# A fused attention and feed-forward kernel: first loads and copies reordered, the last block stored in two halves, and products of the unit matrix on TensorE

## The chip, the cores and the metric

The kernel runs on one core of one Trainium2 chip. That core has five engines, each with its own instruction stream in order: TensorE (PE: products, with PEld for the loads of its stationary operand), VectorE (DVE), ScalarE (ACT), GpSimd (POOL) and SyncE (SP, which here only issues DMA transfers). The metric is device time in microseconds (us) of one execution. Three runs of the kernel before gave a median of 1426.15 us (1426.09 to 1426.85).

## The reference

Attention over 8 batches, 8 heads, 576 positions and 64 features, with a threshold on the scores, and then a two-layer feed-forward network over the 4608 rows of 512 features:

```python
scores = scale * np.matmul(q, k.transpose(0, 1, 3, 2))
thresh = np.max(scores, axis=-1, keepdims=True) - tau
scores = np.where(scores >= thresh, scores, -1000000000.0)
...
attn = attn / (np.sum(attn, axis=-1, keepdims=True) + 1e-09)
return np.matmul(attn, v).astype(np.float32)
...
h = x @ w_in
g = np.maximum(h, 0.0) + np.log1p(np.exp(-np.abs(h)))
return (g @ w_out).astype(np.float32)
```

All of it is in float32; the two weight matrices (512 x 2048 and 2048 x 512) are given in float64. On TensorE a float32 value is carried as a sum of a high and a low part, so that most products are made three times (high by high, high by low, low by high).

## The kernel before, in words

Attention goes in 32 units, one for each batch and pair of heads, and each unit in nine tiles of 128 rows (288 tiles, numbered g). For a unit the kernel loads k, q and v (`load`, `load_v`), splits k and q into parts (`split_k`, `split_q`, with the helpers `hi_of` and `lo_of`), transposes them on PE (`qkT`, L375 to L383) and copies them from PSUM: keys into `kT`, queries, scaled by `qscale`, into `qT[0]` (`queries`, L396). `qT[1]` holds the same with its two halves of 64 partitions exchanged: by two DVE copies in the first unit (L401), by two DMA transfers in all others (`swap`, L404 and L405). The last 64 rows of each head go through `qkT_rest` and `qm`.

A tile's steps are: `scores` (PE, L442), `row_max` (DVE), `exps` (ACT), `mask` (DVE: the threshold and the row's sum), `weights_T` (PE: transposes of the masked exponentials, L490 to L496), `weights_hi` (ACT) and `weights_lo` (DVE) from PSUM into SBUF, and the products with v (`values`). Tiles before `TG` = 36 transpose into banks of the pool `ps_g`, which has four; later ones into the scores' own bank. The first five units take v whole (L568), the others in parts (L574 to L576).

Beside attention, `prep` converts the weights: each of 32 pieces is loaded (L204, tile `wc_i` or `wc_o`), then ACT takes its absolute value (`first`, L212, tile `wa_i` or `wa_o`), POOL and DVE make float32 of its words, and POOL splits it. One piece is begun every second tile. From tile 41 on, the feed-forward network (`hidden`, L664 to L668; `softplus`; `project`, L732) runs between the steps of the tiles, at a quota for each, in nine chunks of 512 rows; behind the last tile only feed-forward work is left. `project_out` adds a block of 128 rows and 512 columns to its sum on DVE, and `store_out` issues its store on SP (L764).

The order is written out by hand. A string gives the steps of each tile, `PAT0` before tile 36 and `PAT` after; in it T is `weights_T`, h `weights_hi`, l `weights_lo`, R `row_max`, e `exps`, m `mask`, f a part of the feed-forward work, x the preparation of the next unit, S `scores`, v the products of `slow`, w the weights, and p a point. `defer(n, f)` holds a function back for n points. All this gives the order in which instructions are made. A planner then sets the order on each engine by priority (the earlier made, the higher) and by when it reckons each instruction to be ready, so that an instruction can be put ahead of earlier ones; `behind(i, others)` adds an edge that keeps i after the last of `others`.

Of the kernel before, what the change touches and what calls it, by code (L numbers as in the profile page):

```python
# [23 lines left out]
P = 128  # L24
# [8 lines left out]
LAG0 = 5  # L33
PAT = "ThRlefmpfxSvwp"
PAT0 = "RMTeShlfpfxvwp"
WD = 4
ST = (1, 3, 4, 4, 5, 6, 6, 8)
VO = (1, 1, 1, 0)
# [22 lines left out]
def tile_kernel(ctx: ExitStack, tc: tile.TileContext, q, k, v, tau, w_in, w_out, out):  # L61
# [29 lines left out]

    nc.scalar.preload_act_table_set("exp_and_others")

    ones = apool.tile([P, S], F32, tag="R", bufs=1, name="ones")[:, 0:P]
# [7 lines left out]
    tau_sb = cpool.tile([P, 1], F32, name="tau_sb")  # L102
    nc.sync.dma_start(tau_sb, tau.partition_broadcast(P))
    ntau = cpool.tile([P, 1], F32, name="ntau")
    nc.vector.tensor_scalar(out=ntau, in0=tau_sb, scalar1=-1.0, scalar2=None, op0=ALU.mult)
    nc.vector.tensor_tensor(out=ntau, in0=ntau, in1=tau_sb, op=ALU.min)
    qscale = cpool.tile([P, 1], F32, name="qscale")
    nc.vector.tensor_scalar(out=qscale, in0=tau_sb, scalar1=0.0, scalar2=SCALE,
                            op0=ALU.is_ge, op1=ALU.mult)

# [11 lines left out]
    nc.vector.memset(qm.bitcast(F32), 0.0)  # L122

    def hi_of(eng, out_, in_):
        if eng is nc.gpsimd:
            eng.tensor_scalar(out=out_, in0=in_, scalar1=1.0, scalar2=1.0, op0=ALU.mult, op1=ALU.mult)
        elif eng is act:
            eng.copy(out_, in_)
        else:
            eng.tensor_copy(out_, in_)  # L130

    def lo_of(eng, out_, in_, hi):
        eng.tensor_tensor(out=out_, in0=in_, in1=hi.bitcast(F32), op=ALU.subtract)  # L133

# [4 lines left out]
    now = {"p": 0, "tile": 0}  # L139
    masked = []  # L140
    scored = []

    def behind(i, others):
# [25 lines left out]
    def to_f32(src, want, name, then):  # L169
# [124 lines left out]
    for b in range(B):  # L294
        for kind in (("one", "two") if b < NSPLIT else ("all",)):
            for hp in range(NPAIR):
# [17 lines left out]
                units.append(s)  # L314

    def load(s):
        h0 = 2 * s.hp
        s.kn = apool.tile([P, 10, D], F32, tag="nat", bufs=3, name=f"kn_{s.i}")
        s.qn = apool.tile([P, 10, D], F32, tag="nat", bufs=3, name=f"qn_{s.i}")
        for t, src in ((s.kn, k), (s.qn, q)):  # L320
            load_rows(s, t, src)
            if t is s.qn and s.kind == "one":
                continue
            for j in range(2):
                nc.sync.dma_start(t[j * SR:(j + 1) * SR, NC, :], src[s.b, h0 + j, SM:S, :])

    def load_rows(s, t, src):
        nc.sync.dma_start(
            t.rearrange("p (h s) d -> p h (s d)", h=2)[:, :, 0:NC * D],
            src[s.b, 2 * s.hp:2 * s.hp + 2, 0:SM, :].rearrange("h (p c) d -> p h (c d)", c=NC),  # L330
        )

    def load_v(s):
        if s.whole:
            s.vn = apool.tile([P, 10, D], F32, tag="vt", bufs=3, name=f"vn_{s.i}")
        else:
            s.vn = apool.tile([P, 10, D], F32, tag="nat", bufs=3, name=f"vn_{s.i}")
        load_rows(s, s.vn, v)
# [12 lines left out]
    def split_q(s, j):  # L351
        t = apool.tile([P, NC + 1, 2 * D], F32R, tag="q2", bufs=1, name=f"q2_{s.i}_{j}")
        a, z = s.cols.start, s.cols.stop
        if j == 0 and s.kind != "one":
            z += 1
        qj = s.qn[:, j * (NC + 1) + a:j * (NC + 1) + z, :]
        hi_of(s.eng, t[:, a:z, 0:D], qj)
        lo_of(s.eng_lo, t[:, a:z, D:2 * D], qj, t[:, a:z, 0:D])
        s.q2.append(t)
# [10 lines left out]
    def qkT(s, j, n):  # L370
# [10 lines left out]
        for c in cols:  # L381
            src = s.k2[:, j * (NC + 1) + c, :] if n == 0 else s.q2[j][:, c, :]
            nc.tensor.transpose(pr[:, c * P:(c + 1) * P], src, identr)  # L383
        if n == 0:
            s.kT.append(apool.tile([P, S + SR], F32R, tag="kT", name=f"kT_{s.i}_{j}"))
            t = s.kT[j]
            defer(1, lambda: act.copy(t[:, SR:S], ps))
# [6 lines left out]
    def queries(s, t0, t1, ps):  # L394

        act.activation(t0, ps, AF.Copy, scale=qscale)  # L396
        if s.i:
            swap(t0, t1)
            return
        for i, o in ((slice(0, D), slice(D, P)), (slice(D, P), slice(0, D))):  # L400
            vec.tensor_scalar(out=t1[o], in0=ps[i], scalar1=qscale[i], scalar2=None, op0=ALU.mult)  # L401

# [4 lines left out]
    def qkT_rest(s, j, ps):  # L407

        act.copy(
            s.kT[j].rearrange("p (k n) -> p k n", n=SR)[:, 0:NC * 2 + 2:NC * 2 + 1, :],  # L410
            ps[:, j * SR:(j + 1) * SR].unsqueeze(1).to_broadcast([P, 2, SR]),
        )
        if j == 0 and s.kind != "one":
            for m in range(2):
                act.activation(qm[:, 0, m, m * SR:(m + 1) * SR], ps[:, P + m * SR:P + (m + 1) * SR],
                                     AF.Copy, scale=qscale)
            swap(qm[:, 0], qm[:, 1])

# [6 lines left out]
    def scores(s, t):  # L425
# [14 lines left out]
        for m, (lhs, j) in enumerate(parts):  # L440
            for hf in range(2):
                i = nc.tensor.matmul(sp[:, hf, 0:HS], lhs, s.kT[j][:, k0 + hf * HS:k0 + (hf + 1) * HS],  # L442
                                     start=(m == 0), stop=(m == len(parts) - 1))
        scored.append(i)

    def row_max(s, t):
# [6 lines left out]
    def exps(s, t):  # L453
        act.activation(e_all[:, s.half[t], :].rearrange("p (h n) -> p h n", h=2), s.sp[t][:, :, 0:HS],
                             AF.Exp, bias=s.m[t][0], scale=1.0)

    def mask(s, t):
# [12 lines left out]
    def mate(s, t):  # L470
# [4 lines left out]
        return (t + 1, False) if u % 2 == 0 else (t - 1, True)  # L475

    def weights_T(s, t):
        half = s.half[t]
# [72 lines left out]
    def slow_products():  # L551
        if not slow:
            return
        for f in slow[0][:3]:
            behind(f(), scored)
        del slow[0][:3]
# [163 lines left out]
    def project(u, qt, tb):  # L720
        o = ps_g.tile([P, 512], F32, tag="g", name=f"o_{u.n}_{qt}_{tb}")
# [5 lines left out]
        for n, (i, m) in enumerate(steps):  # L727
# [4 lines left out]
            nc.tensor.matmul(o, u.g[fc][m // 2][:, sl], wo[fc][:, m % 2, :], start=(n == 0), stop=(n == 3 * QF - 1))  # L732
            if n == 3 * QF - 1:
                defer(1, lambda: project_out(u, qt, tb, o))
            if (u.n, qt, tb) in early and n == 3 * PAIR - 1:
# [3 lines left out]

    def project_out(u, qt, tb, o):  # L740
        if qt == 0 and tb % 2 == 0:
# [3 lines left out]
        if qt == 0:  # L745
            act.copy(a, o)
        else:
            vec.tensor_tensor(out=a, in0=o, in1=a, op=ALU.add)
        if qt == NFC // QF - 1:
            defer(1, lambda: store_out(u, tb, a))  # L750

    def store_out(u, tb, a):
        t0 = u.t0 + tb * P
        c = 0
        while c < P:
# [5 lines left out]
            else:  # L761
                m = min(S - o, P - c)
                dst = out[b * S + o:b * S + o + m, :]
            nc.sync.dma_start(dst, a[c:c + m, :])  # L764
            c += m
# [187 lines left out]
    u0.eng, u0.eng_lo = eng, nc.gpsimd  # L953
    scores(*tiles[0])
    row_max(*tiles[0])
    exps(*tiles[0])
# [83 lines left out]
```

## Time and profile before

| | us |
|---|---|
| median of three runs | 1426.15 |
| the profiled execution, its own time | 1425.26 |
| its span, first to last instruction | 1423.5 |
| PE busy | 1380.4 |
| DVE busy | 987.5 |
| ACT busy | 846.7 |
| POOL busy | 586.2 |

The profile is of one execution. An engine's busy time is the union of its instructions; PE's products overlap, so that a busy PE is not a PE at its peak, and its rate is read from the distance between the starts of like products. A row of a timeline gives the start and the length in us, the engine, the line, the operation, the tiles written and read, their shapes, a count of instructions merged, and in brackets how long the engine sat idle before and what ended that. Most ACT and DVE instructions carry L156 and most POOL ones L126 or L133, the lines of helpers, and are told apart by their tiles.

### The profile page before, as it was taken

The page shows a single profiled execution, that of the slowest core. Times are in us where ns is not written, and L with a number is a line of the kernel's source. Part 1 is how long each engine was busy: PE and PEld are TensorE (multiplying, and loading weights), DVE is VectorE, ACT ScalarE, POOL GpSimd, SP SyncE. Part 2 cuts the span into 40 slices and gives each one's busy share as a digit, 9 for nine tenths or more (in the row PEclk, how much of TensorE's full clock was granted, in tenths as well). Part 3 has the DMA queues.
Part 4 walks back from the last instruction along what each step waited for, and adds up shares of the span by engine and source line. Part 5 has one row for each costly group of instructions (what it writes and reads, how often), then busy time and mean ns, then how long its engine had stood idle before and what let it go on. Part 6 is the DMA issues. An engine that isn't in the chain of part 4 may idle for free.

```text
span 1423.5 us, 23587 instructions
## 1 busy us (share of the span) xinstructions
PE 1380.4 (97%) x7860; PEld 1164.5 (82%) x7860; DVE 987.5 (69%) x2211; ACT 846.7 (59%) x1615; POOL 586.2 (41%) x619
## 2 busy tenths in 40 slices
PE   6987999999999999999999999999999999999998
PEld 5555688788888888888888888888888888788886
DVE  6988688787777777787778777877777777402111
ACT  5766767667666576667666666667666765221110
POOL 3666666543333433344334333344334431323221
PEclk9999999999999999999999999999999999999999
DMA  5766766435333534445443533453434532343421
GB/s 168 220 191 208 233 195 186 125 102 173 111 105 111 156 105 124 120 131 158 118 119 98 158 108 110 124 145 117 123 113 141 154 94 84 110 130 115 135 76 45
DMA packets 131209, 189.94 MB, mean 133 GB/s; under 512 B 35312, under 2 KB 86800, under 8 KB 131088
## 3 DMA queue, kind: packets, MB, share of 16 engines
q1 hardware_dynamic: 131088, 188.43, 45.4%
q8 instruction: 63, 1.03, 0.3%
q14 instruction: 58, 0.48, 0.1%
HBM read 140.51 MB, written 27.41 MB: 118 GB/s over the span
## 4 chain that ended last, share of the span: by engine, by line
PE 86%; DVE 4%; DMA 2%; issue 2%; POOL 2%; ACT 1%; SPq 1%; POOLq 0%; DVEq 0%; ACTq 0%
PE o L732 28%; PE s L442 11%; PE h L664 9%; PE h L666 9%; PE h L668 9%; PE s L493 7%; PE pv L574 4%; PE pv L575 4%; PE tr L383 2%; DVE e_all L156 1%; PE pv L576 1%; DVE negm L156 1%; PE s L490 1%; PE pv L568 1%; DMA wc_i<-in_moe_w_in_dram 1%
## 5 line engine op out<-in xcount | busy, mean ns | idle before, releaser
L732 PE MATMUL o<-wo_o,g 128*128 128x512 f32 x1728 | 446.4, 400 | 1.1 <-POOL g L133 1.1
L732 PEld LDWEIGHTS o<-wo_o,g 128*128 128x128 f32 x1728 | 313.7, 189 | 60.6 <-POOL g L133 2.1
L133 POOL TENSOR_TENSOR g<-st,g 128x512 fp32r<-128x512 f32 x144 | 189.8, 1338 | 240.4 <-DVE g L156 222.4
L156 DVE SCALAR_TENSOR_TENSOR e_all<-s,thr,e_all 128x576 f32<-128x576 f32 x288 | 235.2, 817 | 38.0 <-ACT e_all L156 33.4
L156 ACT CAST gH<-s 128x512 fp32r<-128x512 f32 (+2 forms) x432 | 179.5, 467 | 136.8 <-PE s L493 115.5
L156 ACT ACTIVATE e_all<-s,negm 128x576 f32<-128x576 f32 x288 | 215.8, 750 | 32.7 <-DVE negm L156 17.0
L664 PE MATMUL h<-xh,wi 128*128 128x512 f32 x576 | 232.6, 404 | 1.8 <-ACT xh L156 0.8
L156 DVE TENSOR_REDUCE negm<-s 128x1 f32<-128x576 f32 x288 | 215.2, 747 | 25.0 <-PE s L442 21.9
L666 PE MATMUL h<-xl,wi 128*128 128x512 f32 x576 | 231.6, 402 | 0.7 <-POOL xl L133 0.7
L668 PE MATMUL h<-xh,wi 128*128 128x512 f32 x576 | 229.2, 398 | 0.0
L156 DVE TENSOR_TENSOR gL<-s,gH 128x512 fp32r<-128x512 f32 (+1 forms) x270 | 169.0, 634 | 47.3 <-ACT gH L156 40.5
L442 PE MATMUL s<-kT,qT 128*128 128x288 f32 x1024 | 193.0, 311 | 8.1 <-ACT gH L156 4.1
L156 DVE CAST g<-st 128x512 fp32r<-128x512 f32 x128 | 58.8, 501 | 169.0 <-ACT st L156 169.0
L442 PEld LDWEIGHTS s<-kT,qT 128*128 128x128 f32 x1024 | 148.4, 191 | 24.6 <-ACT gH L156 5.3
L493 PE MATMUL s<-identr,e_all 128*128 128x128 f32 x1008 | 151.3, 273 | 0.2 <-DVE e_all L156 0.2
L156 ACT ACT_TABLE_LOAD x111 | 142.4, 1283 | 5.4 <-PE h L668 3.4
L156 ACT ACTIVATE st<-h 128x512 f32<-128x512 f32 x144 | 78.3, 595 | 112.5 <-PE h L668 111.8
L664 PEld LDWEIGHTS h<-xh,wi 128*128 128x128 f32 x576 | 108.5, 188 | 25.7 <-ACT xh L156 1.3
L493 PEld LDWEIGHTS s<-identr,e_all 128*128 128x128 f32 x1008 | 119.4, 140 | 10.9 <-DVE e_all L156 3.5
L666 PEld LDWEIGHTS h<-xl,wi 128*128 128x128 f32 x576 | 108.6, 188 | 22.2 <-POOL xl L133 1.5
L668 PEld LDWEIGHTS h<-xh,wi 128*128 128x128 f32 x576 | 108.5, 188 | 22.1
L574 PE MATMUL pv<-gH,vt 128*128 128x256 f32 (+1 forms) x432 | 118.3, 297 | 0.3 <-ACT gH L156 0.2
(94 smaller groups left out, 1830.0 us busy)
## 6 DMA issues: line engine op xcount, KB each, us to landing
wi<-wi_d SPq DMA_DIRECT2D x144, 512.0 KB
qT<-qT SPq DMA_DIRECT2D x124, 128.0 KB
R<-r_d SPq DMA_DIRECT2D x64, 144.0 KB
kn<-in_k_dram SPq DMA_DIRECT2D x32, 256.0 KB
qn<-in_q_dram SPq DMA_DIRECT2D x32, 256.0 KB
vn<-in_v_dram SPq DMA_DIRECT2D x32, 256.0 KB
wc_i<-in_moe_w_in_dram SPq DMA_DIRECT2D x16, 512.0 KB
wi_d<-wc_i SPq DMA_DIRECT2D x32, 256.0 KB
```

The lines of the kernel that those rows point to most:

```text
L133: eng.tensor_tensor(out=out_, in0=in_, in1=hi.bitcast(F32), op=ALU.subtract)
L156: i = getattr(self.eng, name)(*args, **kwargs)
L383: nc.tensor.transpose(pr[:, c * P:(c + 1) * P], src, identr)
L442: i = nc.tensor.matmul(sp[:, hf, 0:HS], lhs, s.kT[j][:, k0 + hf * HS:k0 + (hf + 1) * HS], start=(m == 0), stop=(m == len(parts) - 1))
L490: nc.tensor.transpose(rest, e_all.rearrange("p h n -> p (h n)")[:, SM:SM + P], ident)
L493: nc.tensor.matmul(main[:, c, :], e[:, c0:c0 + P], ident, is_transpose=True, start=True, stop=True)
L574: nc.tensor.matmul(o[:, 0:n], vt[:, c, :], h[:, c, 0:n], start=(c == 0), stop=False)
L575: nc.tensor.matmul(o[:, 0:n], vt[:, c, :], l[:, c, 0:n], start=False, stop=False)
L664: nc.tensor.matmul(h, wi[:, 0, cc, :], u.h[cc], start=(cc == 0), stop=False)
L666: nc.tensor.matmul(h, wi[:, 0, cc, :], u.l[cc], start=False, stop=False)
L668: nc.tensor.matmul(h, wi[:, 1, cc, :], u.h[cc], start=False, stop=(cc == NCC - 1))
L732: nc.tensor.matmul(o, u.g[fc][m // 2][:, sl], wo[fc][:, m % 2, :], start=(n == 0), stop=(n == 3 * QF - 1))
```

## The change

- In front, eight products of the unit matrix with itself (repeated over 512 columns) are put on PE before the first loads, two more behind tile 0's scores, and ahead of the transposes of tiles 0, 2, 5, 14, 19, 23, 27, 30, 32 and 33 between one and five each (`KEEP`, `in_use`). They write banks that are overwritten by what comes next, and use no data but the unit matrix.
- Unit 0's q is loaded through ACT's DMA queue, k through SP's. The load of tau goes behind them, and so does the preload of ACT's function table; the values worked out from tau come behind the split of q's first half.
- Unit 0's first queries are scaled and copied in two pieces, 128 and 384 columns. Its second half of the queries uses the two DMA transfers of `swap` in place of the two DVE copies.
- Unit 0's last 64 rows of keys for the first head of the pair are copied on DVE, not ACT; its last queries are held back by three points.
- Edges: the weights' first step on ACT stays behind an exponential of the first two tiles; the second split of q stays behind the first queries.
- From tile 36 on, the point at a tile's end moves behind the next tile's T, h and R.
- The very last block of the output is made as two blocks of 256 columns, each with its own sum and store; where a store is in two pieces, the second is issued on ACT's queue.

```diff
-PAT = "ThRlefmpfxSvwp"
+PAT = "ThRplefmpfxSvw"
+KEEP = {0: 1, 2: 5, 5: 3, 14: 2, 19: 2, 23: 4, 27: 2, 30: 4, 32: 2, 33: 2}
...
-    nc.scalar.preload_act_table_set("exp_and_others")
...
-    nc.sync.dma_start(tau_sb, tau.partition_broadcast(P))
...
+    def load_tau():
+        nc.sync.dma_start(tau_sb, tau.partition_broadcast(P))
+
+    def tau_values():
+        behind(nc.vector.tensor_scalar(out=qscale, in0=tau_sb, scalar1=0.0, scalar2=SCALE,
+                                       op0=ALU.is_ge, op1=ALU.mult), swapped)
...
         def first():
-            act.activation(m, high.bitcast(F32), AF.Abs, scale=2.0 ** 16)
+            i = act.activation(m, high.bitcast(F32), AF.Abs, scale=2.0 ** 16)
+            behind(i, exped[:2])
...
         for t, src in ((s.kn, k), (s.qn, q)):
-            load_rows(s, t, src)
+            eng = nc.sync if s.i or t is s.kn else act
+            load_rows(s, t, src, eng)
...
+        hi = hi_of(s.eng, t[:, a:z, 0:D], qj)
+        lo = lo_of(s.eng_lo, t[:, a:z, D:2 * D], qj, t[:, a:z, 0:D])
+        if not s.i and j:
+            behind(hi, lead)
+            behind(lo, swapped)
+        elif not s.i:
+            swapped.append(lo)
...
-            defer(1, lambda: queries(s, t[0][:, w], t[1][:, w], ps[:, w]))
+            ws = [w] if s.i or j else [slice(0, P), slice(P, SM)]
+            defer(1, lambda: [queries(s, j, t[0][:, w], t[1][:, w], ps[:, w]) for w in ws])
...
-        act.activation(t0, ps, AF.Copy, scale=qscale)
-        if s.i:
+        i = act.activation(t0, ps, AF.Copy, scale=qscale)
+        if s.i or j:
             swap(t0, t1)
             return
+        lead.append(i)
...
-        act.copy(
-            s.kT[j].rearrange("p (k n) -> p k n", n=SR)[:, 0:NC * 2 + 2:NC * 2 + 1, :],
+        hi_of(act if s.i or j else vec,
+              s.kT[j].rearrange("p (k n) -> p k n", n=SR)[:, 0:NC * 2 + 2:NC * 2 + 1, :],
...
+            defer(0 if s.i else 3, lambda: last_queries(ps))
...
+    def in_use(out_, n):
+        for _ in range(n):
+            i = nc.tensor.matmul(out_, identr, identr.unsqueeze(1).to_broadcast([P, 4, P]), start=True, stop=True)
+            behind(i, at_PE)
+            at_PE.append(i)
...
+        in_use(main.rearrange("p c n -> p (c n)"), KEEP.get(now["tile"], 0))
...
+        very = u is chunks[-1] and qt == nq - 1 and tb == u.T // P - 1
+        parts = [slice(0, DM // 2), slice(DM // 2, DM)] if very else [slice(0, DM)]
+        for w, n, (i, m) in [(w, n, x) for w in parts for n, x in enumerate(steps)]:
...
+            eng = act if c and w.stop - w.start < DM else nc.sync
+            eng.dma_start(dst[:, w], a[c:c + m, w])
...
+    in_use(ps_g.tile([P, 512], F32, tag="g", name="first"), 8)
     load(u0)
+    load_tau()
+    behind(act.preload_act_table_set("exp_and_others"), lead)
...
     split_q(u0, 0)
+    tau_values()
...
     scores(*tiles[0])
+    in_use(ps_g.tile([P, 512], F32, tag="g", name="second"), 2)
```

More of the change, by code (lines that the diff above doesn't have):

```diff
@@ L386, in qkT @@
             t = s.kT[j]
-            defer(1, lambda: act.copy(t[:, SR:S], ps))
+            defer(1, lambda: behind(act.copy(t[:, SR:S], ps), [] if s.i else lead[-1:]))
         else:
@@ L407, in qkT_rest, with last_queries @@
     def qkT_rest(s, j, ps):
-        act.copy(
-            s.kT[j].rearrange("p (k n) -> p k n", n=SR)[:, 0:NC * 2 + 2:NC * 2 + 1, :],
-            ps[:, j * SR:(j + 1) * SR].unsqueeze(1).to_broadcast([P, 2, SR]),
-        )
+        hi_of(act if s.i or j else vec,
+              s.kT[j].rearrange("p (k n) -> p k n", n=SR)[:, 0:NC * 2 + 2:NC * 2 + 1, :],
+              ps[:, j * SR:(j + 1) * SR].unsqueeze(1).to_broadcast([P, 2, SR]))
         if j == 0 and s.kind != "one":
[L414 to L417, printed above, removed]
+            defer(0 if s.i else 3, lambda: last_queries(ps))
+    def last_queries(ps):
+        for m in range(2):
+            behind(act.activation(qm[:, 0, m, m * SR:(m + 1) * SR], ps[:, P + m * SR:P + (m + 1) * SR],
+                                        AF.Copy, scale=qscale), lead)
+        swap(qm[:, 0], qm[:, 1])
     e_all = cpool.tile([P, 2, S], F32, name="e_all")
@@ L453, in exps @@
     def exps(s, t):
-        act.activation(e_all[:, s.half[t], :].rearrange("p (h n) -> p h n", h=2), s.sp[t][:, :, 0:HS],
+        i = act.activation(e_all[:, s.half[t], :].rearrange("p (h n) -> p h n", h=2), s.sp[t][:, :, 0:HS],
                              AF.Exp, bias=s.m[t][0], scale=1.0)
+        if not s.i:
+            exped.append(i)
     def mask(s, t):
@@ L554, in slow_products @@
         for f in slow[0][:3]:
-            behind(f(), scored)
+            i = f()
+            behind(i, scored)
+            at_PE.append(i)
         del slow[0][:3]
@@ L747, in project_out, with store_out @@
         else:
[L748 removed]
+            vec.tensor_tensor(out=a[:, w], in0=o[:, w], in1=a[:, w], op=ALU.add)
         if qt == NFC // QF - 1:
[L750 to L752 removed]
+            defer(1, lambda: store_out(u, tb, a, w))
+    def store_out(u, tb, a, w):
         t0 = u.t0 + tb * P
```

54 lines of the change are left out of this document (29 added, 25 removed).

## The prediction

> **What bounds the kernel now.** I read the page first, then the table of stretches, then the timelines of the first 26 us and of the end, because the change touches almost nothing but those two ends.
>
> ```profile
> span 1423.5 us, 23587 instructions
> PE 1380.4 (97%) x7860; PEld 1164.5 (82%) x7860; DVE 987.5 (69%) x2211; ACT 846.7 (59%) x1615; POOL 586.2 (41%) x619
> PEclk9999999999999999999999999999999999999999
> ```
>
> The span is 1423.5 us; the profiled execution's own time is 1425.26 us, so 1.76 us lie around the span, and the median of the runs shown, 1426.15, is 0.89 above that execution. TensorE (PE) is the bound, and the granted clock shows no loss anywhere. By stretches:
>
> ```profile
> 10.00:15.00 5.00, 2.39 (x10) 1.70 (x9) 4.09 (x7) 1.99 (x4) 3.62 (x4) 1.00 0.51 153
> 15.00:20.00 5.00, 3.77 (x17) 3.74 (x17) 2.85 (x8) 2.04 (x6) 0.76 (x2) 1.00 0.90 270
> 50.00:60.00 10.00, 7.65 (x48) 5.25 (x46) 9.63 (x21) 8.25 (x21) 6.94 (x10) 1.00 0.82 227
> 130.00:240.00 110.00, 102.79 (x565) 78.43 (x564) 85.76 (x176) 81.24 (x156) 74.47 (x81) 1.00 0.69 209
> 240.00:500.00 260.00, 258.08 (x1541) 222.71 (x1540) 204.71 (x468) 171.15 (x322) 108.60 (x117) 1.00 0.43 125
> ```
>
> Columns are PE, PEld, DVE, ACT and POOL busy, then clock, DMA share, GB/s. From 240 us on PE has work without a break (258.08 of 260). So time can be won only where PE still waits, ahead of 240 us, and after its last product. The first 36 tiles, which carry no feed-forward work, run at the pace of a loop through PE, DVE and ACT, with DVE nearly full (9.63 of 10); if that loop starts earlier, the saturated part starts earlier and the end moves by the same amount. Now PE in front:
>
> ```profile
> 9.14 1.33 PE L442 MATMUL s<-kT,qT 128*128 128x288 f32 x4 [0.21 <-ACT qT L156]
> 10.69 1.09 PE L442 MATMUL s<-kT,qT 128*128 128x288 f32 x3 [0.22 <-DVE qT L156]
> 16.23 1.11 PE L493 MATMUL tm<-identr,e_all 128*128 128x128 f32 x4 [3.62 <-DVE e_all L156]
> 17.00 1.31 PE L442 MATMUL s<-kT,qT 128*128 128x288 f32 x4
> 21.82 0.66 PE L493 MATMUL tm<-identr,e_all 128*128 128x128 f32 x4 [1.58 <-DVE e_all L156]
> 25.43 0.78 PE L442 MATMUL s<-kT,qT 128*128 128x288 f32 x4
> ```
>
> The same four score products take 1.33 or 1.31 us before 20 us and 0.78 later, the same four transposes 1.11 and 0.66. TensorE runs at about half speed until it speeds up between 17 and 22 us, although the clock row shows full grant. What holds tile 0 and tile 2 stands on ACT and DVE:
>
> ```profile
> 4.69 0.67 ACT L156 CAST k<-kn 128x576 fp32r<-128x576 f32 x1 [2.68 <-DMA kn<-in_k_dram]
> 6.39 0.46 ACT L156 CAST q<-qn 128x320 fp32r<-128x320 f32 x1 [1.03 <-DMA qn<-in_q_dram]
> 8.39 0.70 ACT L156 ACTIVATE qT<-tr,qscale 128x512 fp32r<-128x512 f32 x1
> 9.12 1.51 DVE L156 TENSOR_SCALAR qT<-tr,qscale 64x512 fp32r<-64x512 f32 x2 [1.75 <-ACT qT L156]
> 11.57 0.76 DVE L156 TENSOR_REDUCE negm<-s 128x1 f32<-128x576 f32 x1 [0.48 <-PE s L442]
> 13.44 1.51 DVE L156 TENSOR_SCALAR qT<-tr,qscale 64x512 fp32r<-64x512 f32 x2
> 15.35 0.82 DVE L156 SCALAR_TENSOR_TENSOR e_all<-s,thr,e_all 128x576 f32<-128x576 f32 x1
> 17.96 0.67 ACT L156 ACTIVATE wa_i<-wc_i 128x512 f32<-128x512 f32 x1 [3.73 <-DMA wc_i<-in_moe_w_in_dram]
> 19.97 0.78 ACT L156 ACTIVATE e_all<-s,negm 128x576 f32<-128x576 f32 x1
> 22.28 0.66 ACT L156 ACTIVATE wa_i<-wc_i 128x512 f32<-128x512 f32 x1 [1.53 <-DMA wc_i<-in_moe_w_in_dram]
> 22.85 0.72 ACT L156 ACTIVATE e_all<-s,negm 128x576 f32<-128x576 f32 x1
> ```
>
> Two things are to be seen. The first mask (15.35) waits for copies of q. And ACT, which works in order, stands 3.73 and 1.53 us before the first two weight pieces land; the exponentials of tiles 2 and 3 (19.97 and 22.85) are queued behind those.
>
> **The change part by part.** *First loads.* q's three issues leave SP for ACT's queue, the broadcast of tau goes behind k's three, and the table load goes behind ACT's three. SP's own queue, and the load:
>
> ```profile
> 0.73 0.39 SPq L103 DMA_DIRECT2D tau_sb<-in_tau_dram  x1
> 2.89 0.59 SPq L328 DMA_DIRECT2D qn<-in_q_dram  x1
> 3.52 1.12 SPq L325 DMA_DIRECT2D qn<-in_q_dram  x2
> 10.95 0.50 SPq L404 DMA_DIRECT2D qm<-qm  x1
> 11.49 0.59 SPq L405 DMA_DIRECT2D qm<-qm  x1
> 13.50 0.59 SPq L204 DMA_DIRECT2D wc_i<-in_moe_w_in_dram  x1
> 0.72 1.28 ACT L92 ACT_TABLE_LOAD   x1 [0.72 <-PEq L1024]
> ```
>
> k starts 0.45 us earlier (0.39 and the gap behind it). q no longer lands 1.7 us behind k, so ACT takes it right after k: 4.69 − 0.45 + 0.67 = 4.9 in place of 6.39, and q's transposes gain about 1.0 because DVE's low part of k is still ahead of q's. The table load, started after some 1.7 us of issues, still ends before k lands (ACT idles 2.68 us there); without that cover it would cost its 1.28. tau is issued about 1.7 later, at 2.4, still 6 us ahead of the scaling at 8.39; its three short operations on DVE move behind q's low part.
>
> *Queries.* Only the first 128 of 512 columns are scaled and copied before tile 0's scores. The copies fall from 1.51 to between 0.38 (by columns) and 0.8 (mostly fixed cost), the 0.70 activation likewise; I take 0.5 for the copies. With the earlier q the second pair of score products moves from 10.69 to about 8.4, and the reduction from 11.57 to about 9.1, −2.5.
>
> *Second half of the queries by DMA.* The 1.51 us at 13.44 leaves DVE, where the threshold and both first masks are queued behind it: −1.5 more, together −4.0 at the mask of 15.35. The two new swaps cost SP 0.50 + 0.59; their first reader, tile 5's scores, comes after 25.43, so their landing is covered. The rest of k's copy moves from ACT to DVE, and the last queries wait three points longer: tile 4's scores need them between 21.82 and 25.43, covered as well.
>
> *Clock.* If the eight products and what follows raise it, each of the first two tiles saves 1.11 − 0.66 + 1.31 − 0.78 = 0.98 us. The compute chain then reaches tile 2's exponential some 5.5 us earlier; without the clock 4.0.
>
> *What stops it.* ACT's first two weight waits stay. First piece: 21 SP issues stand ahead of it, 0.73 to 13.50, 0.61 each. q's three go; the qm and query swaps wait on ACT until about 11 us, so the planner can fill in the weight piece ahead of all four (qm's two stand ahead now): 16 issues ahead, −3.0. If the swaps stand in front instead, only three are saved and two added, −0.6. Second piece: its issue is also 0.6 earlier, and 0.5 MB of the first is moved into 10 to 15 us, where DMA carries 153 GB/s against 270 after: another 0.5 MB / 270 = 1.9, so −2.5. I take −2.8 for the front, the mean of these, since tile 2 hangs on the first and tile 3 on the second. Bounds are −0.6 and −5.5.
>
> *Products at ten tiles.* There are 27.
>
> ```profile
> 1396.70 22.11 PE o L732 x96
> 85.13 0.63 PE L493 MATMUL tm<-identr,e_all 128*128 128x128 f32 x4 [1.74 <-DVE thr L156]
> 56.19 0.63 PE L493 MATMUL tm<-identr,e_all 128*128 128x128 f32 x4
> ```
>
> A product of 512 columns is 22.11/96 = 0.23. They run ahead of the transposes, which wait for the mask. Tile 2's five (1.15) fit in the 1.58 at 21.82, tile 23's four (0.92) in the 1.74 at 85.13. Tile 14 (56.19) has no wait: its two cost PE 0.46, in a stretch where PE has 2.35 of 10 free. I take +0.2; with every cover gone it is 27 × 0.23 = +6.2. They add no speed, since the rows after 21.82 are at full pace.
>
> *Points.* From tile 36 on, the point at a tile's end runs after the next tile's transposes, copies and reduction. PE never lacks work there; I take 0. Bounds: −2 (a part of the 7.2 us PE is idle between 130 and 240) and +6.3 (below).
>
> *Last block.*
>
> ```profile
> 1418.84 0.69 DVE L156 TENSOR_TENSOR acc<-o,acc 128x512 f32<-128x512 f32 x1 [2.03 <-PE o L732]
> L764 SPq DMA_DIRECT2D out_dram<-acc x8: 466/531/599, 1411.4 to 1420.1; - x8
> 10.67 0.43 DVE L156 TENSOR_TENSOR q<-qn,q 128x256 fp32r<-128x256 f32 x1
> 182.53 0.28 PE L574 MATMUL pv<-gH,vt 128*128 128x256 f32 x1
> 182.65 0.28 PE L575 MATMUL pv<-gL,vt 128*128 128x256 f32 x1
> ```
>
> Products of 256 columns start 0.12 apart (182.53, 182.65), so 24 of them take 2.9 against 12 × 0.23 = 2.8: +0.1. The add falls from 0.69 to 0.43 (the 256-column row): −0.26. The second store's issue, 0.53, runs on ACT beside the first: −0.53. Behind the last issue (1420.1 + 0.6 = 1420.7) 2.8 us of landing and closing remain. Sum −0.7; between 0, if the issues hinder each other, and −1.0.
>
> **Sum:** −2.8 + 0.2 + 0 − 0.7 = −3.3 on 1425.26, 1421.96 for such an execution; for the median 0.89 more, 1422.9.
>
> A rule speaks against the clock step. By the Trainium skill, "TensorE: Matmul & The Clock Gate", Part 1 (What's actually happening), the clock is raised after one busy window of about 3.4 us, and the windows run freely, not from the kernel's start. The trace agrees in kind: the rows at 16.23 and 17.00 are slow, and that at 21.82 is fast. By the page the eight products (an estimate: 512 columns at 1.2 GHz are 0.43 us, 3.4 in all) fill a window only if it begins with them. It would leave the sum (4.0 is still beyond the 2.8 that the weights let through) and makes the second rival below less likely.
>
> **Rivals.** *The weights hardly come earlier.* The swaps stand in front of the first piece on SP, and the front brings −0.6: −0.6 + 0.2 − 0.7 = −1.1, 1425.0. For: SP has no break before 13.50, so whatever it issues first delays the rest. Against: a queue filled in the planner's order of readiness need not hold a piece that waits for nothing.
>
> *The whole compute chain comes through.* The planner puts the exponentials of tiles 2 and 3 ahead of the weight step: −5.5 + 0.2 − 0.7 = −6.0, 1420.2. For: the new edge keeps the weight step behind the first exponentials. Against: it names no later ones, and the clock must be raised early.
>
> *Slower: PE waits for a PSUM bank.* What is deferred at a tile's end (evacuation of the transposed k and q, of values and sums) now stands on ACT and DVE behind the next tile's copies and reduction (0.76 at 11.57), while PE has four such banks. The gain of 3.3 is gone once each of 252 tiles loses 0.013 us; at 0.025 the loss is 6.3, and 1422.9 + 6.3 = 1429.2. Against: DVE has 204.71 of 260 busy and ACT 171.15, and PE hardly waited in that stretch.
>
> **How the numbers follow.** Forecast 0.44, weights 0.20, whole chain 0.24, bank 0.12. The likeliest alone spans 1421.4 to 1424.4. The range reaches from 1419.0, below the whole chain's time, to 1427.0, beyond the weights' rival; most of the bank's case and a sliver of the chain's are left out. A measurement of this kernel tells about 0.2% (2.9 us) from no change, so faster means below 1423.3: the whole chain, and somewhat over half of the forecast's case, 0.50. Slower is the bank, 0.12. The rest, 0.38, is within.
>
> **What would show it.** Right: the first score pair's second half near 8.4; the first mask near 11.3; ACT's first weight step near 15 and its second near 19.7; score quartets at 0.78 from about 10 us; the last store's issue alongside another on ACT, and 2.8 us behind it. Wrong: a first weight issue still past 12.5 on SP; the tile 2 exponential ahead of the weight step; score quartets still at 1.3; PE waits in 240 to 500 above 1.92 us. Above all the forecast falls if the tile rate of the first 36 changes beyond the first five, since I let the front's gain pass through it unaltered.

## The result, and the profile after

| | us |
|---|---|
| before, median of 5 runs | 1426.85 (1426.09 to 1430.54) |
| after, median of 5 runs | 1481.85 (1480.17 to 1484.14) |
| after over before | 1.0381, 95% interval 1.0365 to 1.0396 |
| after, the profiled execution, its own time | 1484.14 |

The change makes the kernel 55 us slower; 1422.9 was forecast, and the range ended at 1427.0. The page of the kernel after, its busy times and then rows of its costliest groups (busy us, mean ns of one | idle us of the engine ahead of them, and what ended most of it):

```profile
span 1482.4 us, 23626 instructions
PE 1423.6 (96%) x7909; PEld 1166.3 (79%) x7909; DVE 982.2 (66%) x2213; ACT 848.8 (57%) x1615; POOL 583.5 (39%) x619
...
L773 PE MATMUL o<-wo_o,g 128*128 128x512 f32 (+1 forms) x1740 | 451.0, 400 | 19.3 <-ACT qm L162 17.5
L162 ACT CAST gH<-s 128x512 fp32r<-128x512 f32 (+2 forms) x432 | 179.3, 463 | 362.8 <-PE s L528 292.1
...
L162 DVE SCALAR_TENSOR_TENSOR e_all<-s,thr,e_all 128x576 f32<-128x576 f32 x288 | 235.2, 817 | 119.3 <-ACT e_all L162 112.8
```

The same groups on the page of the kernel before:

```profile
L732 PE MATMUL o<-wo_o,g 128*128 128x512 f32 x1728 | 446.4, 400 | 1.1 <-POOL g L133 1.1
...
L156 DVE SCALAR_TENSOR_TENSOR e_all<-s,thr,e_all 128x576 f32<-128x576 f32 x288 | 235.2, 817 | 38.0 <-ACT e_all L156 33.4
L156 ACT CAST gH<-s 128x512 fp32r<-128x512 f32 (+2 forms) x432 | 179.5, 467 | 136.8 <-PE s L493 115.5
```

The instructions of these groups didn't become longer (463 ns for 467, 817 for 817). What grew is standing still: ACT ahead of its copies of the transposed weights (gH) by 226 us, DVE ahead of the masks by 81, and PE's products into o wait 17.5 us for a copy into `qm`, for which they never waited before. PE's busy time grew by 43.2 of the 58.9 us of the span, with only 49 products more. It is the union of records that overlap, and products that start further apart overlap less, so most of PE's loss is not shown as idle. Where the time goes is seen by stretches (columns as in the prediction). First the kernel after, from 240 us on, and behind it two stretches of the kernel before (its 240 to 500, 258.08 with 1541 products, stands in the prediction):

```profile
240.00:500.00 260.00, 249.12 (x1452) 207.91 (x1452) 193.88 (x442) 161.84 (x306) 106.47 (x116) 1.00 0.41 118
500.00:750.00 250.00, 243.37 (x1424) 205.65 (x1424) 180.65 (x418) 160.90 (x297) 92.08 (x97) 1.00 0.42 121
750.00:1000.00 250.00, 244.18 (x1436) 207.20 (x1435) 186.03 (x429) 153.09 (x288) 93.94 (x100) 1.00 0.42 119
```

```profile
500.00:750.00 250.00, 249.58 (x1504) 219.33 (x1503) 192.61 (x444) 169.66 (x316) 98.05 (x104) 1.00 0.43 125
750.00:1000.00 250.00, 249.72 (x1502) 219.62 (x1501) 193.93 (x446) 163.69 (x307) 97.33 (x102) 1.00 0.43 123
```

In equal time PE does 1452 products for 1541, 1424 for 1504, 1436 for 1502: 4 to 6% fewer, everywhere, at a clock of 1.00 in both. So the loss is spread over the tiles, not made in one place. The starts of the masks say the same: against the kernel before, that of tile 41 comes 0.5 us earlier, tile 72's 7.6 later, tile 180's 37.3, tile 287's 58.5. None of it is ahead of tile 41. Of the 8 us up to tile 72, more than half come between tiles 42 and 45, where this execution has 6.83 us at half clock; the other 51 are 0.24 us for each tile.

How a tile loses it is seen in the timeline of the kernel after (start, length, engine and so on; in brackets the engine's idle time and what ended it):

```profile
852.91 0.23 PE L393 MATMUL tr<-identr,k 128*128 128x128 f32 x1
852.97 0.23 PE L395 MATMUL tr<-identr,q 128*128 128x128 f32 x1
...
853.19 0.74 ACT L162 ACTIVATE e_all<-s,negm 128x576 f32<-128x576 f32 x1
...
854.90 0.61 PE L528 MATMUL s<-identr,e_all 128*128 128x128 f32 x4
...
855.54 0.58 ACT L162 CAST gH<-s 128x512 fp32r<-128x512 f32 x1 [1.61 <-PE s L528]
856.02 0.27 ACT L162 CAST kT<-tr 128x128 fp32r<-128x128 f32 x1
...
856.18 0.53 ACT L162 ACTIVATE qm<-tr,qscale 128x64 fp32r<-128x64 f32 x2
...
856.77 1.20 PE L773 MATMUL o<-wo_o,g 128*128 128x512 f32 x4 [1.02 <-ACT qm L162]
```

k and q are transposed into a bank (`tr`) by 853.20, and ACT is free at 853.93. But its next instruction in order is the next tile's copy into gH, whose transposes PE does only at 854.90. ACT stands for 1.61 us with the evacuation of `tr` ready behind it, and does it from 856.02 on, some 2 us late. PE's next product o reads nothing from `qm`; it needs one of the four banks of `ps_g`. That the one it gets is this one is read from the kernel's code and from the times: the copy out of it ends at 856.71, and o starts at 856.77, after a wait of 1.02 us. In the kernel before, the evacuations stand ahead of the copy into gH:

```profile
786.69 0.59 ACT L156 CAST kT<-tr 128x512 fp32r<-128x512 f32 x1 [2.23 <-PE s L442]
787.18 0.69 ACT L156 ACTIVATE qT<-tr,qscale 128x512 fp32r<-128x512 f32 x1
787.76 0.59 ACT L156 CAST gH<-s 128x512 fp32r<-128x512 f32 x1
```

By the Trainium skill, "Perfetto Trace Analysis", Optimizing Tensor Performance (Matmuls), independent groups of products should rotate through different PSUM banks, so that the evacuation of one overlaps the products of the next. Both kernels rotate through the same four banks; the 1.02 us shows that this was not enough where the evacuation stands in its engine's order behind something that is not ready.

### The profile page after: what moved, and what is told of

Its sections match the earlier page's. It is cut to its first block, busy times and chain, and to the rows that moved or that the text cites. A ratio compares the mean times of both kernels' runs of the same rounds, so it can differ in the third digit from the quotient of the medians.

```text
span 1482.4 us, 23626 instructions
## 1 busy us (share of the span) xinstructions
PE 1423.6 (96%) x7909; PEld 1166.3 (79%) x7909; DVE 982.2 (66%) x2213; ACT 848.8 (57%) x1615; POOL 583.5 (39%) x619
## 4 chain that ended last, share of the span: by engine, by line
PE 72%; ACT 10%; DVE 9%; issue 4%; DMA 3%; POOL 2%; SPq 0%; ACTq 0%; POOLq 0%; DVEq 0%
PE o L773 18%; PE s L466 10%; PE h L705 8%; PE h L703 8%; PE h L701 8%; PE s L528 7%; PE pv L611 4%; PE pv L612 4%; ACT gH L162 3%; DVE e_all L162 2%; ACT L162 2%; DVE negm L162 2%; ACT e_all L162 2%; PE tr L401 2%; DVE gL L162 2%
## 5 line engine op out<-in xcount | busy, mean ns | idle before, releaser
L773 PE MATMUL o<-wo_o,g 128*128 128x512 f32 (+1 forms) x1740 | 451.0, 400 | 19.3 <-ACT qm L162 17.5
L701 PE MATMUL h<-xh,wi 128*128 128x512 f32 x576 | 233.8, 406 | 4.0 <-ACT xh L162 3.4
L705 PE MATMUL h<-xh,wi 128*128 128x512 f32 x576 | 234.0, 406 | 0.0
L528 PE MATMUL s<-identr,e_all 128*128 128x128 f32 x1008 | 154.7, 276 | 1.7
L528 PEld LDWEIGHTS s<-identr,e_all 128*128 128x128 f32 x1008 | 114.8, 141 | 24.8 <-DVE e_all L162 16.8
L649 POOL TENSOR_TENSOR xp<-xp,R 128x576 f32<-128x576 f32 x32 | 46.0, 1437 | 207.8 <-DMA R<-r_d 195.9
L162 DVE CAST g<-st 128x512 fp32r<-128x512 f32 x128 | 51.4, 444 | 111.6 <-ACT st L162 111.6
```

The lines of the kernel that those rows point to most:

```text
L162: i = getattr(self.eng, name)(*args, **kwargs)
L528: nc.tensor.matmul(main[:, c, :], e[:, c0:c0 + P], ident, is_transpose=True, start=True, stop=True)
L649: nc.gpsimd.tensor_tensor(out=s.xp[:, 0:s.n], in0=s.xp[:, 0:s.n], in1=s.R[:, 0:s.n], op=ALU.mult)
L701: nc.tensor.matmul(h, wi[:, 0, cc, :], u.h[cc], start=(cc == 0), stop=False)
L705: nc.tensor.matmul(h, wi[:, 1, cc, :], u.h[cc], start=False, stop=(cc == NCC - 1))
L773: nc.tensor.matmul(o[:, w], u.g[fc][m // 2][:, sl], wo[fc][:, m % 2, w], start=(n == 0), stop=(n == 3 * QF - 1))
```

## The experiments

The theory from here on: the whole loss comes from the place of the point (p) in a tile's steps. The rivals: that the products of the unit matrix, or the changes in front, cost it.

**1. The change with the old place of the point.**

```diff
-PAT = "ThRplefmpfxSvw"
+PAT = "ThRlefmpfxSvwp"
```

> The changed kernel with the points of every tile put back to where they were; all else of the change stays. Theory A (the points alone cost the time: from tile 81 to tile 270 the changed kernel loses 40 us, 2.1 to 2.3 in each unit of nine tiles, at unchanged work): between 1421 and 1428 us, masks 81 to 270 as far apart as before (777 us). Rival B (the new front gives the planner another order all the way down, and the points are innocent): still above 1460 us. Rival C (the products keep PE busy at the wrong times): no more than a few us can come of 35 products, so C alone can't give the 55.

Measured: 1424.12 us (1421.82 to 1427.69, ten runs) beside 1427.23 of the kernel before (25 runs): 0.998, interval 0.9968 to 0.9993. PE no longer waits for `qm`, and the masks of tiles 81 and 270 lie 814.8 us apart, for 814.9 in the kernel before and 857.7 in the kernel after (the 777 above is not their distance). All that was lost comes back, and what is left of the change gains about 3 us.

**2. The kernel before, with nothing but the new place.**

```diff
-PAT = "ThRlefmpfxSvwp"
+PAT = "ThRplefmpfxSvw"
```

> The kernel before with the new points and nothing else. Theory A: 1480 to 1486 us, with a wait of about 1.0 us once per unit ahead of the output products for the copy of the last queries on ACT. Rival B: 1424 to 1430 us.

Measured: 1484.09 us (four runs), 1.0398, interval 1.0374 to 1.0422: +57 us from this string alone. Its waits between 400 and 1200 us (us in total, times, longest) are those of the kernel after:

```profile
ACT gH L156 <- PE s L493: 236.2, 122, 3.2
...
DVE e_all L156 <- ACT e_all L156: 75.6, 80, 1.5
...
PE o L732 <- ACT qm L156: 15.5, 15, 1.0
```

The two rivals are out: neither a product nor a load is changed here.

**3 and 4. The old place, without any of the unit matrix's products, and with those in front alone.** Both are experiment 1 with

```diff
-KEEP = {0: 1, 2: 5, 5: 3, 14: 2, 19: 2, 23: 4, 27: 2, 30: 4, 32: 2, 33: 2}
+KEEP = {}
```

and experiment 3 also leaves out the two calls of `in_use` in front.

> The changed kernel with the old points and without any product of the unit matrix. If the products do nothing for the clock (it rose only at 17 us with them, 20 without), within 1.5 us of the run with them. If they are what keeps the clock up, more spells at half clock than with them, and about 3 us for each.

> The changed kernel with the old points, with the eight products in front and the two behind tile 0's scores, without those at the ten tiles. If the ten tiles' products keep the clock up, spells at half clock appear behind the longest idle stretches of PE among the first 34 tiles, about 3 us each; if not, the time is that of the run with them, within 1.5 us.

Measured: 1426.7 us without any (ten runs; 1.0001, interval 0.9985 to 1.0017) and 1427.66 with those in front (ten runs; 0.9999, interval 0.9984 to 1.0013), against 1424.12 with all. Both are further from it than the 1.5 us that was expected of products that do nothing. This leans towards the products at the ten tiles being worth some 2 or 3 us, but the intervals overlap, and the granted clock doesn't bear it out: its mean over the runs is 0.997 with all and without any, 0.995 with those in front, and the profiled executions have one stretch at half clock, two, and none. Experiment 12 tries it again.

**5, 6 and 7. Which of the late functions costs it.** The kernel before with the new place of the point, and at the tile's end a second, partial point (q) that runs only deferred functions of one kind: in experiment 5 the evacuations of transposed k and q, in 6 those of the products with v (`values_out`), in 7 the feed-forward network's (`softplus`, the parts, `project_out`, `store_out`).

```diff
-PAT = "ThRlefmpfxSvwp"
+PAT = "ThRplefmpfxSvwq"
...
-            defer(1, lambda: qkT_rest(s, j, ps))
+            defer(1, lambda: qkT_rest(s, j, ps), "k")
...
-        defer(1, lambda: values_out(s, g, o))
+        defer(1, lambda: values_out(s, g, o), "v")
...
+    def early_point():
+        now["p"] += 1
+        due = [x for x in later if x[0] <= now["p"] and x[2] and x[2] in EARLY]
...
+        now["p"] -= 1
```

> The kernel before with the new points, but the copies of the transposed keys and queries out of PSUM stay at the old place, the tile's end. Theory A1 (PE waits for a bank that holds transposed keys and queries, since ACT stands, in order, ahead of the next tile's copies while those of keys and queries are ready behind them: 1.0 us at PE once per unit, and the exponentials behind them late): at least half of the 57 us comes back, 1455 us or less. Rival A2 (the sums of the products with v are what comes late: DVE's mask and low parts stand behind them): 1475 us or more.

> The same, with only the copies of the products with v at the old place. A1: 1470 us or more. A2: 1455 us or less.

> The same, with only the feed-forward work's deferred steps (softplus with its splits, and the sums and stores of the output) at the old place. A1 and A2: 1470 us or more. A third case, that the hidden layer's banks are what is held: 1450 us or less.

Measured, one run each: 1463.71, 1463.12 and 1481.09 us (1429.33 for the kernel before beside them). Of the 57 us, the transposed k and q early bring back 20, the values early 21, the network 3. So neither A1 nor A2 met its numbers for experiments 5 and 6: each kind carries a part. Waits of experiment 5, then of 6 (400 to 1200 us):

```profile
ACT gH L157 <- PE s L494: 216.8, 131, 3.2
...
DVE e_all L157 <- ACT e_all L157: 30.1, 45, 1.3
```

```profile
ACT gH L157 <- PE s L494: 215.8, 139, 2.7
...
DVE e_all L157 <- ACT e_all L157: 69.2, 65, 1.5
...
PE o L733 <- ACT qm L157: 11.9, 15, 0.8
```

PE's wait for `qm` is gone in experiment 5 and stays in 6, as it should if each takes away its own late evacuation. DVE's wait ahead of the masks falls to 30.1 with 20 us won in the one and stays at 69.2 with 21 us won in the other, so that wait doesn't carry the loss. ACT's own wait stays at 216 in both.

What PE loses, and where, is seen in the starts of its products. Between the masks of tiles 60 and 280, take from each distance of two starts the usual one behind a product of that shape, and add up what is over by the product that comes next (us; below the first row, against the first row):

| | the whole stretch | ahead of o | ahead of the scores | ahead of the weights' transposes |
|---|---|---|---|---|
| before | 946.3 | 6.6 | 16.4 | 35.2 |
| experiment 2 | 1000.6 | +26.7 | +18.0 | +7.6 |
| 5, k and q early | 977.0 | +1.9 | +20.8 | +8.4 |
| 6, values early | 975.2 | +19.7 | +2.0 | +3.8 |
| 10, both early | 946.1 | +0.3 | −1.8 | +2.5 |

So there are two ways to lose, and each kind takes away one. Late copies of k and q hold a bank of `ps_g`, and the sums o wait for it (in experiment 2, 21.7 us in 17 waits that the copy into `qm` ends). Late values make DVE late, and the scores wait until DVE has read their own bank for the last time (its step into gH ends 71 waits, 19.8 us in all; in experiment 6, 2 waits and 0.6 us). How the values make DVE late is a reading: their sum on DVE waits for ACT's copy, and DVE's later work is queued behind it.

**10. Both kinds early.** `EARLY = "kv"` on the same base.

> The kernel before with the new points, but both the copies of transposed keys and queries and those of the products with v at the old place. Alone they brought back 20 and 21 us of 57. If they are two separate delays on the same engine they add up: 1440 to 1446 us. If what remains is shared between them: 1434 us or less.

Measured, one run: 1433.41 us beside 1427.09 of the kernel before. 50 of the 57 us are back, 9 more than the 20 and 21 of the two alone. Single runs that spread by 6 us and more can't tell that from nothing. In the table, k and q alone bring back 23.6 of 54.3 us, the values alone 25.5, and both together all of it: in the main two separate delays, with some 5 us that either one is enough to cause. ACT's wait falls as well:

```profile
ACT gH L157 <- PE s L494: 116.9, 136, 2.4
```

The 6 us that remain are not made at these tiles (946.1 us for 946.3). Its masks are 8.3 us late at tile 60 already, in an execution whose clock rose at 25.58 us (19.99 in that of the kernel before) and which has 6.83 us at half clock behind 155.28. So the network's functions at the new place cost nothing that shows there.

**8, 9 and 11. Which of the three steps in front of the point costs it.** The change, with the point behind T, ahead of the copies (8, and 11 timed), or behind h, ahead of the reduction (9).

```diff
-PAT = "ThRplefmpfxSvw"
+PAT = "TphRlefmpfxSvw"
```

```diff
-PAT = "ThRplefmpfxSvw"
+PAT = "ThpRlefmpfxSvw"
```

> The changed kernel with the point between the next tile's transposes and its copies (TphRle...), not behind copies and reduction. A1: what ACT stands before is the copy (h); with the point ahead of it the evacuations go first and nearly all comes back: below 1432 us. If it is the transposes on PE that come too early, or the planner's priorities in general, still above 1450.

> The changed kernel with the point behind the next tile's copies, ahead of its reduction (ThpRle...). If the copies on ACT are what the evacuations must not stand behind: most of the 57 us lost again, above 1460 us. If DVE's reduction is: below 1435 us.

> The changed kernel with the point behind the next tile's transposes, timed. Its one look gave 1421.9; expected 1421 to 1425 in the median, 2 to 5 us below the kernel before beside it.

Measured: behind T 1421.9 in a single run, and 1425.52 (1422.81 to 1429.28, eleven runs) beside 1427.09 (21 runs): 0.9988, interval 0.9976 to 0.9999. That is 1.6 us below it and not the 2 to 5 expected; the single run was lower than all eleven. Behind h, one run: 1579.28. One letter, h, stands between the two, and it costs 154 us (its profiled execution has eleven stretches of 3.41 us at half clock, which can make up to 19 of them). Waits of experiment 8, 400 to 1200 us:

```profile
ACT gH L162 <- PE s L528: 81.6, 109, 1.2
...
DVE e_all L162 <- ACT e_all L162: 14.3, 25, 0.8
```

81.6 is what the kernel before has, 82.5 by the same view. So it is the copies (h) ahead of the evacuations that cost the time. That the point behind R (1481.85) is cheaper than behind h was not foreseen. The timeline of experiment 9 shows why, as a reading and not as a test of its own:

```profile
801.14 0.86 ACT L162 CAST gH<-s 128x512 fp32r<-128x512 f32 x2 [1.99 <-PE s L528]
...
802.02 0.37 ACT L162 COPY xp<-pv 64x256 f32<-64x256 f32 x1
...
802.42 0.43 DVE L162 TENSOR_TENSOR xp<-pv,xp 64x256 f32<-64x256 f32 x1 [1.82 <-ACT xp L162]
...
802.88 0.76 DVE L162 TENSOR_REDUCE negm<-s 128x1 f32<-128x576 f32 x1
...
803.67 0.74 ACT L162 ACTIVATE e_all<-s,negm 128x576 f32<-128x576 f32 x1 [1.28 <-DVE negm L162]
```

ACT stands 1.99 us for the transposes, with the evacuation of the values behind it. DVE's part of that evacuation waits 1.82 us for ACT's, and now the reduction is queued behind it, and ACT's exponential waits for the reduction. With the point behind R, the reduction at least goes ahead.

One condition was not varied. In both kernels, from tile 72 on (`TQ` in the code, class `Queue`), each instruction of ACT and of DVE is kept behind the one made before it; up to there the planner may still put a ready one ahead. The masks of experiment 9, against the kernel before, come 0.2 us earlier at tile 48, 2.0 later at tile 72, 10.5 at tile 76 and 154.2 at tile 287; those of experiment 2 come 4.2, 9.1, 13.3 and 59.8 later. So the steady loss begins where the written order is binding. Whether the planner alone would have avoided the rest, no run shows.

**12. The point behind T, without any product of the unit matrix.** The edit of experiment 8 together with that of 3.

> The same without any product of the unit matrix. If the products bring nothing: within 1 us of the run with them, and the same mean clock (with the old points it was 0.997 with and without). If they bring the 2.6 us between the two medians with the old points: 1424 to 1427.

Measured: 1426.25 us (1423.16 to 1429.05, eleven runs), 0.9993, interval 0.9984 to 1.0003, against 0.9988 with the products, beside the same runs of the kernel before. The difference of 0.7 us leans the same way as before and is well inside the intervals, and 1426.25 lies in both of the expected ranges. Whether the products are worth anything stays open.

Best of what was measured are the change with the old place of the point (0.998) and with the point behind T (0.9988); their intervals overlap.

## Why the prediction was wrong, and where it was right

**The step that failed** is "Points": "PE never lacks work there; I take 0." It is +57 us (experiment 2), and the prediction's own sign of it came true: PE stands for 260 − 249.12 = 10.88 us between 240 and 500, where above 1.92 was to mean wrong. The bound of +6.3 came from the third rival, "Slower: PE waits for a PSUM bank", which the experiments bear out in kind: the evacuations deferred at a tile's end stand behind the next tile's copies, and PE waits for banks, those of `ps_g` and the scores' own. Its size was nine times too small, because it was set by the gain it would have to undo and not by a row. Rows of the kernel before gave a warning. ACT has 171 of 260 us busy, and that average was taken for slack. But ACT works in order, and its row for gH above shows it idle for 115.5 us in front of these copies, until PE has made their transposes; whatever is put behind such a copy is late by the wait, however much ACT idles. And PE was the bound, with four banks for transposes, values, feed-forward sums and outputs, so that it missed a bank that was freed 2 us late (the 1.02 us at 856.77). How much PE would lose in all can't be read from these rows. The rival's own text also named the copies and the reduction as one thing; experiments 8 and 9 show that the copies alone cost it, and that, with the copies ahead, the reduction ahead of the evacuations is a help.

**The rest of the change** was forecast at −3.3 us and is worth 1424.12 − 1427.23 = −3.1 by experiment 1 and −1.6 by experiment 11, with intervals of −4.6 to −1.0 and −3.4 to −0.1. The size is borne out as far as these intervals go. Without the products, which were taken to bring nothing, it is −0.5 (experiment 3) and −0.8 (experiment 12), so which part brings what is open. Several steps were wrong, and that the sum comes near is in part luck. First PE, ACT, DVE and SP of the kernel after in front:

```profile
5.53 0.67 ACT L162 CAST k<-kn 128x576 fp32r<-128x576 f32 x1 [1.67 <-DMA kn<-in_k_dram]
6.10 0.45 ACT L162 CAST q<-qn 128x320 fp32r<-128x320 f32 x1
...
8.99 0.71 DVE L162 TENSOR_SCALAR qT<-tr,qscale 64x128 fp32r<-64x128 f32 x2 [0.62 <-ACT qT L162]
...
11.07 0.59 SPq L210 DMA_DIRECT2D wc_i<-in_moe_w_in_dram  x1
11.44 1.25 DVE L162 TENSOR_SCALAR qT<-tr,qscale 64x384 fp32r<-64x384 f32 x2
...
14.30 0.81 DVE L162 SCALAR_TENSOR_TENSOR e_all<-s,thr,e_all 128x576 f32<-128x576 f32 x1
...
15.58 0.68 ACT L162 ACTIVATE wa_i<-wc_i 128x512 f32<-128x512 f32 x1 [0.17 <-DMA wc_i<-in_moe_w_in_dram]
...
17.55 0.77 PE L466 MATMUL s<-kT,qT 128*128 128x288 f32 x4
...
18.38 1.52 ACT L162 ACTIVATE e_all<-s,negm 128x576 f32<-128x576 f32 x2
18.41 0.58 SPq L210 DMA_DIRECT2D wc_i<-in_moe_w_in_dram  x1
...
23.13 0.70 ACT L162 ACTIVATE wa_i<-wc_i 128x512 f32<-128x512 f32 x1 [1.79 <-DMA wc_i<-in_moe_w_in_dram]
```

- *First loads*: wrong. k was to be taken at 4.24 and came at 5.53, later than the 4.69 before; q does follow k at once, but at 6.10 and not 4.9. In the eight profiled executions with the new loads k is taken at 4.92 to 5.53, in the six with the old ones at 4.69 to 4.90, though it is issued 0.45 us earlier. The prediction took it that an earlier issue lands earlier.
- *Queries*: half right. The small copies cost 0.71, not 0.5, and the first reduction starts at 10.65 (9.1 forecast, 11.57 before).
- *Second half of the queries by DMA*: wrong. The 1.51 us left DVE, as said, but the other 384 columns of the first half now stand ahead of the mask, 1.25 us at 11.44, which the sum left out. So the first mask came at 14.30, 1.05 earlier and not 4.0.
- *What stops it*: the first piece of the weights was issued at 11.07 (10.5 forecast) and taken at 15.58 (15 forecast, 17.96 before): right. The second was issued later than before (18.41 for 15.78) and taken at 23.13 for 22.28, not at 19.7: wrong. It didn't matter, since the planner put the exponentials of tiles 2 and 3 (18.38) ahead of it, as the second rival had it. The masks of tiles 2 and 3 come 1.8 and 3.2 us earlier than before. At tile 35, up to which the point is the same in all kernels, the mask starts at 119.5 to 124.7 us in the eight profiled executions with the new front, 122.1 in the mean, and at 122.8 to 125.3 in the six with the old one, 124.2 in the mean: −2.1, where the front and the products at the tiles were to bring −2.6. So about that is gained, by another way, and single executions spread by more than the gain.
- *Clock*: quartets of scores were to run at 0.78 from about 10 us. They do from 17.55 on; the first fast row of the kernel before is that of 21.82. The eight products in front didn't bring it in this execution (more on that below). The prediction's own terms, 4.0 and two of 0.98, also make 6.0 and not its 5.5.
- *Products at ten tiles*: +0.2 was taken; whether it is a little more or a gain, the runs don't tell.
- *Last block*: −0.7 forecast. From the end of the last product (1418.80 before, 1417.63 in experiment 4) to the end of the span (1423.5 and 1421.2) it is 4.7 us before and 3.6 in experiment 4, −1.1. All eight profiled executions with the split block have 3.54 to 3.56 there, all six without it 4.68 to 4.69. Behind the last product −0.79 was forecast; the bound for the whole was −1.0. The add and the issues, in the timeline of experiment 4:

```profile
1416.68 1.94 ACTq L162 DMA_DIRECT2D out_dram<-acc  x2
1417.66 0.42 DVE L162 TENSOR_TENSOR acc<-o,acc 128x256 f32<-128x256 f32 x1 [1.01 <-PE o L773]
```

The add is 0.42 for 0.69, and the last issue ends at 1416.68 + 1.94 = 1418.62, 2.6 us ahead of the span's end, for 2.8.

## What to carry to other kernels

On an engine that works in order, and where the written order is binding, an average of idle time is no slack: ask of every instruction that is moved behind another what that other waits for, and who waits for the moved one. Evacuations of PSUM that are ready belong ahead of copies whose source is still to be made, above all where the bound engine rotates through few banks. And a risk that a prediction names wants its price from a row (here ACT's 115.5 us of standing in front of the copies), not from what would just undo the gain.

## What the runs showed of the hardware

**Two loads on two queues come closer together, and the first of them not earlier.** With q on ACT's queue beside k on SP's, k is taken at 4.92 to 5.53 and not at 4.69 to 4.90, q at 5.50 to 6.10 and not at 6.20 to 6.39. That k now shares the DMA engines with q would explain it, and so would v, whose first issue moves from 4.68 to 3.12; neither was tried alone.

**The clock is granted in steps of 3.41 us, and falls within a busy kernel.** In every trace here the time between two changes of the clock is a multiple of 3.413 us (for example 37.55, 6.83, 92.16). Experiment 11 shows the whole cycle in front. Windows of its clock's steps (PE busy first, clock third from the end), and then PE's rows:

```profile
2.45:5.86 3.41, 3.04 (x8) 1.83 (x6) 0.00 (x0) 1.73 (x2) 0.00 (x0) 1.00 0.77 227
5.86:9.27 3.41, 2.12 (x18) 1.75 (x18) 2.44 (x8) 1.83 (x6) 0.00 (x0) 1.00 0.54 133
9.27:16.10 6.83, 5.37 (x20) 4.31 (x21) 4.98 (x11) 3.78 (x9) 3.55 (x5) 0.50 0.79 230
```

```profile
8.43 0.53 PE L466 MATMUL s<-kT,qT 128*128 128x288 f32 x2
9.18 1.46 PE L466 MATMUL s<-kT,qT 128*128 128x288 f32 x4 [0.22 <-DVE qT L162]
```

Here the clock rose at 5.86, with only the eight products in front on PE so far, and at 9.27 it was halved again, after a stretch in which PE was busy for 2.12 of 3.41 us. (The 1.00 ahead of 5.86 is not the clock that PE ran at: that is the first change of it on record, and products of 512 columns start 0.43 us apart before it, 0.23 at 17.36.) In the other executions with these products the first rise came at 16.55 to 17.99, after the dense stretch that begins near 13; without them at 18.31 to 25.58. By the Trainium skill, "TensorE: Matmul & The Clock Gate", Part 1 (What's actually happening), the gate closes after an idle window of about 3.4 us; here it closed after that stretch, so a window needn't be idle for it. In all 14 traces the clock falls 33 times ahead of the last product, each time behind 3.41 us in which PE was busy for 0.12 to 2.12 us, and never behind more; some stretches of 1.56 to 2.12 us were followed by no fall. The kernel after shows the price of such a fall in the middle of its first 36 tiles, its stretch at half clock and the one behind:

```profile
54.64:61.47 6.83, 6.25 (x19) 3.65 (x17) 5.01 (x10) 3.89 (x12) 5.78 (x7) 0.50 0.61 169
61.47:68.30 6.83, 6.70 (x39) 4.37 (x39) 5.10 (x13) 4.29 (x9) 2.12 (x2) 1.00 0.47 126
```

19 products in place of 39, at nearly the same busy share. In experiment 1 the lead over the kernel before is 2.65 us at tile 42 and 0.14 at tile 45, around a stretch of 3.41 us at half clock from 153.09. Such stretches come in 12 of the 14 profiled executions, at differing places; in experiment 4's profiled one there is none, and it took 1423.0, while that kernel's other runs took up to 1430.97. In experiment 1 the fastest of ten runs has a mean clock of 1.000 (1421.82), the two slowest 0.994 (1426.54 and 1427.69). So they are part of why the runs of one kernel spread over some 6 to 9 us, which is more than the gain that was forecast. They are not all of it: experiment 11 loses some 2 us between tiles 48 and 53 at full clock, and why was not pursued.
